# One load cut in two, and two early products put behind the head matmuls, in a one-token attention block

## The chip, the core and the metric

The kernel runs on one NeuronCore of a Trainium2 chip. The core has five engines that run side by side and meet at semaphores: TensorE (PE) for matmuls, VectorE (DVE), ScalarE (ACT), GpSimd (POOL) and SyncE (SP), which here only issues transfers. Sixteen DMA engines carry data between the chip's main memory and the on-chip tile memory of 128 partitions. The metric is the device time of one execution in microseconds (us). The times of before are 1310.05 us as the median of three runs (1310.01 to 1310.16).

## The reference

One token of each of two sequences is decoded. The input is layer-normed. One branch is attention of 32 query heads over 8 cached key/value heads, each with 32,768 positions of 128 numbers; the other is a small gated feed-forward. Their product is added to the input.

```python
xn = layernorm(x)                                   # x: 2 x 1 x 512
q = (xn @ wq).reshape(B, 1, 32, 128)                # wq: 512 x 4096
k, v = repeat(k_cache, 4), repeat(v_cache, 4)       # caches: 2 x 8 x 32768 x 128, float32
p = softmax(einsum("bhqd,bhkd->bhqk", q, k) * 128 ** -0.5)
s = einsum("bhqk,bhkd->bhqd", p, v).reshape(B, 1, 4096) @ wo      # wo: 4096 x 512
gate = xn @ W_gate                                  # 512 x 1792
h = gate * (gate > 0) * (xn @ W_up)
out = x + s * silu(h @ W_down)                      # W_down: 1792 x 512
```

Everything is float32. The caches are two times 268 MB, and each number of them is used once.

## The kernel before

The caches are read in loads of 8 MB: a load is one row of 16,384 numbers (64 KB) for each of the 128 partitions. The two sequences and eight key/value heads make 16 groups; a group is four tiles of 8,192 positions, and a load brings two tiles. So there are 32 loads of keys (tiles `k0` and `k1` by turns) and 32 of values (tile `w`, which the code calls `wide`; the last but one goes into `k0`).

The step `j` of the main loop (L882) works on one pair of tiles. DVE turns the keys in 32 by 32 blocks (L660), PE multiplies them by the query (`s<-k,qcur`), DVE takes the scores (L678), ACT exponentiates a whole group (L722), PE and DVE bring the weights into the layout that the values need (`pt`, `wt`), and PE sums the values (`o<-w,wt` or `o<-k,wt`) two steps later. At the end of a group, DVE adds the four parts of the sum into `ob` (L771, L777), four head matmuls (`m_ps<-ob,heads`) spread it by heads, DVE turns that (L803), and POOL stores it in `ots` (L812), where the heads of all groups stand until the projection by `wo`.

Nothing sets the order at run time. The `Program` class records each operation with the tiles that it reads and writes (by key), and works out from these which semaphore each operation waits for; within an engine the order is that of the recording. All large loads stand on SP's queue. `load` (L239) records a transfer with a semaphore of its own name, and a load into a tile waits until the last readers of its key are through.

The beginning. The first operation of all (L261) is the load of the query weights `wq`, 8 MB, into `w`; the second is the first load of keys. ACT's queue loads `x` twice, 4 KB each (L289, L290). DVE and POOL prepare constants, DVE makes the layer norm (L364 to L380), PE turns it (L391), DVE copies it to `wt0` (L401), and `project_q` (L456) multiplies it by the query weights; it waits for `wt0` and `w`. After that `w` is free for the weights of the feed-forward.

The end. In the last but one step the last values are loaded, and then `load_wo` (L439) brings the output weights into `k1` in six pieces: the first half of `wo` in one piece of 4 MB, the second in pieces of 2 MB, 1 MB, 512 KB, 256 KB and 256 KB, each with its own semaphore. `project_near` (L826) takes the output projection in products of four matmuls, each of the four on its own 32 columns of PE: product `n` needs rows of `ots` and one piece of `wo`. Seven products add up in one bank, `s0`. Products 0 to 3 need the first half of `wo` and heads that were done long before; products 4 to 6 need the heads of the last group too. DVE copies the bank (L846), and `project_far` (L848) adds the remaining pieces of `wo` and the folded copy in a second bank. DVE multiplies by the gate (L870) and adds the input (L872), and SP writes the result.

In the last step the order is this (L911 to L919): `sums`, `take_o` (which makes `ob`), products 0 to 3, `finish_group` (the head matmuls, L803 and L812), and, behind the loop, products 4 to 6 (L936).

## Time and profile before

| what | value |
|---|---|
| median of three runs | 1310.05 us (1310.01 to 1310.16) |
| the profiled execution | 1309.84 us |
| its span, first to last instruction | 1308.2 us |
| mean granted clock of TensorE | 0.836 |
| read from main memory | 564.67 MB, 432 GB/s over the span |
| busy: PE, DVE, ACT, POOL | 65%, 55%, 4%, 1% |
| DMA packets | 10692 |

Times in the profile count from the start of the span. An engine's busy time says how long its instructions took, not that the kernel waited for them: the chain that ended last shows that. A row of a group gives the line, engine, operation, the tile written and those read, the count, the busy time, and what ended the idle time before it. Buffer numbers are left out, so `k` is `k0` or `k1` and `s` one of the two banks of scores, which the end of the kernel uses for the output projection.

### The profile page before, as it was taken

The page shows a single profiled execution, that of the slowest core. Times are in us where ns is not written, and L with a number is a line of the kernel's source. Part 1 is how long each engine was busy: PE and PEld are TensorE (multiplying, and loading weights), DVE is VectorE, ACT ScalarE, POOL GpSimd, SP SyncE. Part 2 cuts the span into 40 slices and gives each one's busy share as a digit, 9 for nine tenths or more (in the row PEclk, how much of TensorE's full clock was granted, in tenths as well). Part 3 has the DMA queues.
Part 4 walks back from the last instruction along what each step waited for, and adds up shares of the span by engine and source line. Part 5 has one row for each costly group of instructions (what it writes and reads, how often), then busy time and mean ns, then how long its engine had stood idle before and what let it go on. Part 6 is the DMA issues. An engine that isn't in the chain of part 4 may idle for free.

```text
span 1308.2 us, 11146 instructions
## 1 busy us (share of the span) xinstructions
PE 850.1 (65%) x4720; PEld 211.5 (16%) x4720; DVE 718.0 (55%) x690; ACT 51.4 (4%) x133; POOL 10.5 (1%) x38
## 2 busy tenths in 40 slices
PE   3566565766666586566667656676665657666676
PEld 0211111111111121111211111121111112111122
DVE  2666654565655456664546666455665545656521
ACT  0001000000000000000000000000000000000000
POOL 0000000000000000000000000000000000000000
PEclk9777888897788888777887878788878888977888
DMA  9999999999999999999999999999999999999998
GB/s 417 419 438 441 439 427 439 429 439 427 439 427 441 427 439 441 429 441 429 435 431 437 429 439 429 437 439 429 443 431 435 431 437 429 439 427 439 435 433 361
DMA packets 10692, 564.79 MB, mean 432 GB/s; under 512 B 1194, under 2 KB 1210, under 8 KB 1596
## 3 DMA queue, kind: packets, MB, share of 16 engines
q1 hardware_dynamic: 10668, 564.67, 99.7%
q8 instruction: 6, 0.10, 0.0%
q14 instruction: 2, 0.02, 0.0%
q10 hardware_dynamic: 16, 0.01, 0.0%
HBM read 564.67 MB, written 0.00 MB: 432 GB/s over the span
## 4 chain that ended last, share of the span: by engine, by line
DMA 63%; DVE 18%; PE 15%; issue 4%; SPq 0%; POOL 0%
DMA k<-in_A_k_cache_dram 58%; DVE k L660 18%; PE o L243 8%; PE s L243 6%; DMA k<-in_A_wo_dram 3%; DMA w<-in_A_wq_dram 2%; PE m_ps L243 1%; PE m_ps L693 0%; SPq L240 0%; DVE os L803 0%; DVE os L846 0%; DVE gy L870 0%; DVE gy L872 0%; POOL ots L812 0%
## 5 line engine op out<-in xcount | busy, mean ns | idle before, releaser
L243 PE MATMUL s<-k,qcur 128*32 128x512 f32 x2048 | 491.5, 687 | 377.0 <-DVE k L660 376.9
L660 DVE STREAM_TRANSPOSE k<-k 128x2048 f32<-128x2048 f32 x256 | 565.2, 2275 | 148.4 <-DMA k<-in_A_k_cache_dram 148.4
L243 PE MATMUL o<-w,wt 128*16 128x512 f32 x1984 | 244.8, 595 | 7.9 <-DMA w<-in_A_v_cache_dram 7.9
L243 PEld LDWEIGHTS s<-k,qcur 128*32 128x32 f32 x2048 | 87.7, 120 | 782.2 <-DVE k L660 645.2
L737 DVE STREAM_TRANSPOSE wt<-pt 128x512 f32<-128x512 f32 x64 | 45.9, 717 | 145.0 <-PE pt L243 140.7
L678 DVE TENSOR_SCALAR_CACHE_REDUCE st<-s 128x512 f32<-128x512 f32 x64 | 43.0, 672 | 113.4 <-PE s L243 113.4
L243 PEld LDWEIGHTS o<-w,wt 128*16 128x16 f32 x1984 | 62.7, 97 | 165.5 <-issue 165.5
L722 ACT ACTIVATE st<-st,nb 128x512 f32<-128x512 f32 x64 | 45.4, 710 | 1109.1 <-DVE nb L719 1109.1
L243 PE MATMUL pt<-st,perm 128*128 128x512 f32 x128 | 75.4, 720 | 1.5 <-ACT st L722 1.5
L763 DVE RECIPROCAL rl<-m_ps 128x1 f32<-128x1 f32 x16 | 2.7, 168 | 109.3 <-PE m_ps L243 109.3
L243 PE MATMUL m_ps<-ob,heads 128*128 128x128 f32 x128 | 21.7, 320 | 29.0 <-DVE ob L777 29.0
L243 PEld LDWEIGHTS pt<-st,perm 128*128 128x128 f32 x128 | 26.0, 225 | 35.0 <-issue 30.7
L803 DVE STREAM_TRANSPOSE os<-m_ps 128x512 f32<-128x512 f32 x16 | 11.5, 717 | 25.6 <-PE m_ps L243 25.6
L243 PEld LDWEIGHTS m_ps<-ob,heads 128*128 128x128 f32 x128 | 18.0, 217 | 31.1 <-DVE ob L777 30.3
L243 PE MATMUL m_ps<-w,wt 128*32 128x512 f32 (+1 forms) x128 | 17.0, 666 | 8.3 <-DMA w<-in_A_wq_dram 8.3
L777 DVE SCALAR_TENSOR_TENSOR ob<-o,share,ob 128x128 f32<-128x128 f32 x48 | 16.9, 351 | 1.7
L530 POOL TENSOR_TENSOR qcur<-qall,block_of 128x128 f32<-128x128 f32 x16 | 6.5, 406 | 1008.4 <-PE s L243 972.6
L243 PE MATMUL o<-k,wt 128*16 128x512 f32 x64 | 9.5, 757 | 4.5 <-DMA k<-in_A_v_cache_dram 4.5
L243 PE MATMUL m_ps<-negone,mrow 1*128 1x1 f32 x32 | 6.0, 256 | 9.3 <-DVE mrow L708 9.3
L722 ACT ACTIVATION_READ_ACCUMULATOR st<-st,nb 128x1 f32 x64 | 12.0, 187 | 0.0
L481 DVE COPY os<-m_ps 128x512 f32<-128x512 f32 x2 | 1.4, 691 | 17.3 <-PE m_ps L243 17.3
L391 PE MATMUL m_ps<-ident,st 32*128 32x32 f32 x4 | 0.7, 308 | 14.0 <-DVE st L380 14.0
(80 smaller groups left out, 103.1 us busy)
## 6 DMA issues: line engine op xcount, KB each, us to landing
k<-in_A_wo_dram SPq DMA_DIRECT2D x1, 4096.0 KB, 39.1
w<-in_B_W_gate_dram SPq DMA_DIRECT2D x1, 3584.0 KB, 18.5
w<-in_B_W_up_dram SPq DMA_DIRECT2D x1, 3584.0 KB, 26.6
w<-in_B_W_down_dram SPq DMA_DIRECT2D x1, 3584.0 KB, 17.3
k<-in_A_wo_dram SPq DMA_DIRECT2D x1, 2048.0 KB, 43.4
k<-in_A_wo_dram SPq DMA_DIRECT2D x1, 1024.0 KB, 45.4
k<-in_A_k_cache_dram SPq DMA_DIRECT2D x32, 48.6
k<-in_A_wo_dram SPq DMA_DIRECT2D x1, 512.0 KB, 46.2
```

The lines of the kernel that those rows point to most:

```text
L243: return lambda e: e.matmul(out_, lhs, rhs, start=start, stop=stop, skip_group_check=True)
L391: lambda e, k=k: e.transpose(px[:, k * 32 : (k + 1) * 32], xquad[:, k, :], ident[:32, :32])
L481: dve(lambda e, q=qs, h=half: e.tensor_copy(q, pq[h]), [f"m{half}"], [f"os{half}"])
L530: lambda e: e.tensor_tensor(qcur.rearrange("p e (k h) -> p e k h", h=REP), qall[:, b, hk].unsqueeze(2).to_broadcast([P, 4, Q // REP, REP]) ...
L660: dve(lambda e: e.transpose(at_, at_), [f"k{t // 2 % 2}"], [key])
L678: lambda e: e.tensor_scalar(st[u], ps_s[t % 2], SCALE, None, op0=ALU.mult, op1=ALU.max, accum_out=mx[:, u : u + 1],),
L722: lambda e, u=u: e.activation(st[u], st[u], AF.Exp, bias=nb, scale=1.0, accum_out=ls[:, u : u + 1]),
L737: dve(lambda e: e.transpose(wt[t % 2], ps_p[t % 2]), [f"pt{t % 2}"], [f"wt{t % 2}"])
L763: dve(lambda e: e.reciprocal(rl, ps_m[1][:, :1]), ["m1"], ["rl"])
L777: lambda e, part=part, c=c: e.scalar_tensor_tensor(ob, part, share[:, c : c + 1], ob, op0=ALU.mult, op1=ALU.add),
L803: lambda e: e.transpose(ot, ps_m[1].rearrange("p (h q j) -> p j h q", h=REP, j=ROWS)),
```

## The change

The load of the query weights becomes two: partitions 0 to 15 with a semaphore `wq0`, and partitions 16 to 127 with the semaphore `wq`. The second writes a key of its own, `wide_rest`, so that it does not wait for the first; `project_q` reads both keys. And in the last step two of the early products, not four, stand ahead of `finish_group`; products 2 and 3 come behind it, with 4 to 6.

```diff
+FIRST = 16
...
-    load(wide, wq.rearrange("(p k) n -> p (k n)", k=NKC), "wq", w=["wide"])
+    wq_rows = wq.rearrange("(p k) n -> p (k n)", k=NKC)
+    load(wide[:FIRST], wq_rows[:FIRST], "wq0", w=["wide"])
+    load(wide[FIRST:], wq_rows[FIRST:], "wq", w=["wide_rest"])
...
-                ["wt0", "wide"],
+                ["wt0", "wide", "wide_rest"],
                 [f"m{half}"],
...
                 take_o()
                 if not live:
-                    project_near(range(4))
+                    project_near(range(2))
                 finish_group(j // 2 - 1)
...
-    project_near(range(4, NEAR))
+    project_near(range(2, NEAR))
     project_far()
```

SP's queue at the start of the program, before (each row is a transfer: tile, source, partitions x numbers):

```order
L240 DMA w<-in_A_wq_dram 128x16384
L240 DMA k<-in_A_k_cache_dram 128x16384
L240 DMA w<-in_B_W_gate_dram 128x7168 [waits sem_PE]
L240 DMA w<-in_B_W_up_dram 128x7168
L240 DMA k<-in_A_k_cache_dram 128x16384
```

The same place after the change, where all lines have moved down by one:

```order
L241 DMA w<-in_A_wq_dram 16x16384
L241 DMA w<-in_A_wq_dram 112x16384
L241 DMA k<-in_A_k_cache_dram 128x16384
L241 DMA w<-in_B_W_gate_dram 128x7168 [waits sem_PE]
L241 DMA w<-in_B_W_up_dram 128x7168
L241 DMA k<-in_A_k_cache_dram 128x16384
```

One row became two, neither of which waits; everything behind stands one place later.

PE at the end of the program, from the sums of the last group on, before (`s<-k,ots` are the products by the output weights, four rows each; `m_ps<-ob,heads` are the head matmuls):

```order
L243 MATMUL m_ps<-lcol,same 128x1 [waits sem_DVE]
L243 MATMUL s<-k,ots 32x512 [waits sem_wo0_0]
L243 MATMUL s<-k,ots 32x512 x15
L243 MATMUL m_ps<-ob,heads 128x128 [waits sem_DVE]
L243 MATMUL m_ps<-ob,heads 128x128 x3
L243 MATMUL s<-k,ots 32x512 [waits sem_wo1_0,sem_POOL]
L243 MATMUL s<-k,ots 32x512 x7
L243 MATMUL s<-k,ots 32x512 [waits sem_wo1_8]
L243 MATMUL s<-k,ots 32x512 x3
```

The same place after the change:

```order
L244 MATMUL m_ps<-lcol,same 128x1 [waits sem_DVE]
L244 MATMUL s<-k,ots 32x512 [waits sem_wo0_0]
L244 MATMUL s<-k,ots 32x512 x7
L244 MATMUL m_ps<-ob,heads 128x128 [waits sem_DVE]
L244 MATMUL m_ps<-ob,heads 128x128 x3
L244 MATMUL s<-k,ots 32x512 x8
L244 MATMUL s<-k,ots 32x512 [waits sem_wo1_0,sem_POOL]
L244 MATMUL s<-k,ots 32x512 x7
L244 MATMUL s<-k,ots 32x512 [waits sem_wo1_8]
L244 MATMUL s<-k,ots 32x512 x3
```

Eight matmuls, which wait for nothing new, went from ahead of the head matmuls to behind them; the products that wait for POOL and the later pieces of `wo` kept their order.

## The prediction

> **What bounds the kernel now.** I read the page first: the share of each engine, the DMA line of the forty slices, and the chain of work that ended last.

> ```profile
> PE 850.1 (65%) x4720; PEld 211.5 (16%) x4720; DVE 718.0 (55%) x690; ACT 51.4 (4%) x133; POOL 10.5 (1%) x38
> DMA  9999999999999999999999999999999999999998
> GB/s 417 419 438 441 439 427 439 429 439 427 439 427 441 427 439 441 429 441 429 435 431 437 429 439 429 437 439 429 443 431 435 431 437 429 439 427 439 435 433 361
> DMA 63%; DVE 18%; PE 15%; issue 4%; SPq 0%; POOL 0%
> ```

> No compute engine is above 65%, while the sixteen DMA engines are at 90% or more in every slice but the last. The DMA share by stage (the last two numbers of each row are that share and the GB/s) makes this sharper:

> ```profile
> 43.00:83.00 40.00, 21.27 (x130) 5.92 (x130) 25.79 (x19) 0.00 (x0) 0.00 (x0) 0.80 1.01 435
> 83.00:640.00 557.00, 372.88 (x2033) 88.24 (x2032) 322.11 (x293) 22.90 (x61) 4.46 (x14) 0.83 1.00 435
> 640.00:1250.00 610.00, 403.44 (x2165) 98.72 (x2169) 349.54 (x314) 22.69 (x63) 4.48 (x15) 0.83 1.00 434
> ```

> From 43 to 1250 us the transfer engines have no hole to give back. 435 GB/s over 16 engines is 27.2 GB/s each. A row of one partition (16384 floats, 65,536 bytes, one packet) so takes 65,536 / 27.2 GB/s = 2.41 us, and a load of 128 rows, eight packets per engine, 19.3 us. Next, how far ahead of need the transfers are issued:

> ```profile
> k<-in_A_k_cache_dram SPq DMA_DIRECT2D x32, 48.6
> w<-in_A_v_cache_dram SPq DMA_DIRECT2D x31, 29.7
> w<-in_A_wq_dram SPq DMA_DIRECT2D x1, 22.1
> ```

> A load of 19.3 us that lands 48.6 or 29.7 us after its issue has stood in the queue behind another for at least 10 us. So time lost by the DMA engines is not made up anywhere: whatever the slowest of them loses at the start comes out at the end, one for one, and so does whatever it gains. I therefore price the first edit in DMA engine time and the second by what waits in the last 13 us.

> **The first load: what it removes.** The packets are counted where they begin; these are the first slices with any (again share and GB/s last):

> ```profile
> 1.50:2.00 0.50, 0.00 (x0) 0.00 (x0) 0.42 (x8) 0.00 (x0) 0.00 (x0) 1.00 3.58 1180
> 2.00:2.50 0.50, 0.00 (x0) 0.00 (x0) 0.20 (x4) 0.00 (x0) 0.00 (x0) 1.00 1.82 655
> 2.50:3.00 0.50, 0.00 (x0) 0.00 (x0) 0.45 (x1) 0.00 (x0) 0.00 (x0) 1.00 0.30 131
> 3.00:3.50 0.50, 0.00 (x0) 0.00 (x0) 0.39 (x2) 0.23 (x1) 0.00 (x0) 1.00 0.33 131
> ```

> 1180 GB/s for 0.5 us is 590 KB, nine packets; then 5, 1 and 1 (131 GB/s is one). So sixteen engines begin one after another, the last some 1.0 to 1.5 us after the first. A first transfer with one packet per engine can let all begin together. Gain: at least 0, at most 1.3 us (the spread). I take 0.3, because fourteen of the sixteen begin within the first us, and the engine that begins last is the last at the end only if no other is held up later.

> **What it adds.** One more DMA on SP's queue, ahead of the first key load:

> ```profile
> 0.74 0.39 SPq L240 DMA_DIRECT2D w<-in_A_wq_dram  x1
> 1.19 0.41 SPq L240 DMA_DIRECT2D k<-in_A_k_cache_dram  x1
> 0.74 22.13 DMA w<-in_A_wq_dram
> 23.01 10.05 PE m_ps L243 x64
> ```

> The key load is issued about 0.45 us later, at 1.64, and its first packet is not due before the query weights are through at about 22.5: 20 us of cover, cost 0. Only with that cover gone would it cost the 0.45. PE waits for one semaphore more ahead of the query projection, which starts when the last part lands; nothing else is queued there that could run. The two small loads of x on ACT's queue share the DMA engines with these packets:

> ```profile
> 10.19 0.67 DVE L364 TENSOR_REDUCE stat<-st 32x1 f32<-32x512 f32 x1 [2.98 <-DMA st<-in_A_x_dram]
> 14.77 0.29 DVE L401 COPY wt<-m_ps 128x128 f32<-128x128 f32 x1 [0.78 <-PE m_ps L391]
> 23.01 10.00 PE L243 MATMUL m_ps<-w,wt 128*32 128x512 f32 x64 [8.28 <-DMA w<-in_A_wq_dram]
> ```

> x arrives by 10.19 and the normalised activations are ready at 15.06, 8 us before the weights. If first packets become longer, x comes later by about as much as the weights, so this stays covered.

> **What it moves: where the sixteen engines write.** This is the term that decides. In every large load of the trace sixteen engines write all 128 partitions at once. In the new first transfer they all write partitions 0 to 15. No row shows such a transfer, so I bound it. From below: each engine is bound by itself, the packet stays at 2.41 us, cost 0. From above: if the tile's way in is shared out by partitions, eight neighbours to a way (the 128 partitions over sixteen engines' worth of rate), sixteen partitions have two ways, eight engines share each, and the first packets take 8 x 2.41 = 19.3 us: 16.9 us lost. Between these, with neighbours in fours the sixteen engines have four ways and lose 3 x 2.41 = 7.2 us; in twos they lose 2.4. No row is near either end; I take 7.2, the rung nearest the middle (8.4) of 0 and 16.9.

> [...]

> The second transfer has 112 rows, seven per engine. From below: as in the whole loads, nobody meets, 0. From above: sixteen neighbours in each of seven steps, 7 x 7.2 = 50.7 us. Between: each engine takes seven rows that lie together, so at any moment the engines stand seven rows apart, in sixteen different fours of the 32. Two fours share a way; the partner of a four is then in use with chance 15/31 = 0.48, and a packet that meets another takes up to 2.41 us more: 7 x 2.41 x 0.48 = 8.2 us. I take 5, nearer to this than to the whole loads' 0, because engines that met fall out of step and meet for part of a packet only. What remains is kept for the range.

> **The two products moved at the end.** These are the rows of the last 13 us, and the landing times of the output weights:

> ```profile
> 1256.35 2.81 SPq L240 DMA_DIRECT2D k<-in_A_wo_dram  x6
> 1295.38 1.12 DVE L777 SCALAR_TENSOR_TENSOR ob<-o,share,ob 128x128 f32<-128x128 f32 x3
> 1295.45 3.64 PE L243 MATMUL s<-k,ots 128*32 128x512 f32 x32 [0.96 <-DMA k<-in_A_wo_dram]
> 1299.02 1.16 PE L243 MATMUL m_ps<-ob,heads 128*128 128x128 f32 x8
> 1300.21 0.72 DVE L803 STREAM_TRANSPOSE os<-m_ps 128x512 f32<-128x512 f32 x1 [3.71 <-PE m_ps L243]
> 1300.99 0.21 POOL L812 COPY ots<-os 32x16 f32<-32x16 f32 x1 [39.64 <-DVE os L803]
> 1301.26 1.50 PE L243 MATMUL s<-k,ots 128*32 128x512 f32 x12 [1.08 <-POOL ots L812]
> 1302.76 0.37 PEld L243 LDWEIGHTS s<-k,ots 128*32 128x32 f32 x8 [0.48 <-DMA k<-in_A_wo_dram]
> 1304.11 0.69 DVE L846 COPY os<-s 128x512 f32<-128x512 f32 x1 [3.18 <-PE s L243]
> 1305.79 0.29 DVE L870 TENSOR_TENSOR gy<-s,gy 128x128 f32<-128x128 f32 x1 [0.99 <-PE s L243]
> k<-in_A_wo_dram SPq DMA_DIRECT2D x1, 2048.0 KB, 43.4
> k<-in_A_wo_dram SPq DMA_DIRECT2D x1, 1024.0 KB, 45.4
> k<-in_A_wo_dram SPq DMA_DIRECT2D x2, 256.0 KB, 46.4
> ```

> ob is done at 1296.50, but the head matmuls wait behind four products and start at 1299.02. A product costs (1299.02 - 1295.45)/4 = 0.89 us. With two ahead the heads start at 1297.24, 1.78 earlier, and POOL has written ots by 1299.42 instead of 1301.20. The two moved products then run from 1298.4 to 1300.2, in PE's old idle time (1.08 us before 1301.26). What is late next is the data. The six issues take 2.81 us, one each 0.476: the 2048 KB piece is issued at 1256.83 and lands at 1300.2, the 1024 KB piece at 1257.30 and lands at 1302.7, the last at 1258.73 and lands near 1305.1. So products five and six run from 1300.2 to 1302.0, and the seventh starts at 1302.76, with its data. Now PE works without a break from 1301.26 to 1304.09, and the seventh starts after two products, at about 1303.0. The copy thus moves from 1304.11 to about 1303.87: 0.24 us at most, and at least 0, if the last pieces bind. I take 0.2.

> **Sum.** +7.2 +5.0 -0.3 -0.2 = +11.7 us on the profiled execution's own 1309.84 (span 1308.2 and 1.6 around it): 1321.5. The median of the runs is 0.2 above that execution, so 1321.7.

> **Rivals.** First, no meeting: the engine alone limits a packet. For it: packets keep their rate in all stages, 434 to 435 GB/s, and nothing in this trace shows a shared way; against it: no row has sixteen engines on few partitions. Then -0.3 -0.2 = -0.5, 1309.5; with the whole start-up spread gone 1308.5; with nothing gained 1310.0. It decides as soon as the 16-row transfer lands within 5 us of its issue. Not slower; chance 0.31, nearly all within 0.2%. It includes the case that the edit does not do what it says, because another engine is last at the end.

> Second, neighbours in twos: +2.4 and little in the second transfer, about 1312.5 (1311.5 to 1316): 0.05.

> Third, the 112 rows are dealt out in turn, so that every step is like the first: +7.2 x 8 = 57.9, 1367.5. For it: nothing; against it: the whole loads are dealt so that nobody meets. 0.06.

> Fourth, faster by over 0.2% (2.6 us): start-up spread and tail together give at most 1.3 + 0.24 = 1.5, so something unseen must help: 0.02.

> **Numbers.** 0.2%, 2.6 us, is about what a measurement of this kernel can tell from no change. The forecast (a loss of 6 to 18 us) has 0.56, and its own range is 1316 to 1328: the first packets alone from below; from above 7.2 + 8.2 and some engine held up besides, or the full 16.9. The whole range runs down to the first rival, 1309.0 to 1328.0, and leaves out about 0.1. Slower: 0.56 + 0.06 + 0.04 of the twos = 0.66; same: 0.30 + 0.02 = 0.32; faster 0.02.

> **What would show it.** In the DMA issues the 1 MB transfer should take about 10 to 12 us to land, not 4 to 5, and the rest of the query weights should land near 34, not 22.9. The first of the forty slices should show about 300 GB/s or less instead of 417, the middle ones 435 as now, and the chain should end with the same pieces later by the same amount. The seventh product should start with its DMA, and the head matmuls right behind the second. A 1 MB transfer that lands in under 5 us makes the forecast wrong; so does a landing of the query weights before 25 us, or a second transfer that takes several times its 17 us.

## The result, and the profile after

The change makes the kernel slower: 1330.88 us (median of five runs, 1330.51 to 1331.85) against 1310.05, a ratio of 1.016 with a 95% interval of 1.0148 to 1.0171. That is 20.8 us more; 11.7 had been forecast, and the range ended at 1328.0.

The page of the changed kernel, as for before: shares of the engines, the DMA line and the rate in forty slices, the chain.

```profile
PE 855.0 (64%) x4720; PEld 211.1 (16%) x4720; DVE 718.2 (54%) x690; ACT 51.4 (4%) x133; POOL 10.5 (1%) x38
DMA  9999999999999999999999999999999999999998
GB/s 217 364 433 445 434 426 436 440 432 428 438 436 436 426 438 436 436 430 436 434 440 432 432 434 438 436 428 436 438 434 428 438 436 436 428 438 434 436 430 346
DMA 64%; DVE 18%; PE 14%; issue 4%; SPq 0%
```

The DMA engines are as busy as before in every slice, yet in the first (33 us long) they move 217 GB/s instead of 417: busy, but at half speed. From the third slice to the last but one the rates lie where they lay (426 to 445 GB/s, against 427 to 443 before), and the stage from 83 to 640 us has its share of 1.00 and 434 GB/s, against 435:

```profile
83.00:640.00 557.00, 371.29 (x1993) 89.45 (x1989) 318.61 (x285) 22.15 (x58) 4.08 (x13) 0.82 1.00 434
```

So the loss lies at the start, and what is lost there is carried to the end. The chain over the first 80 us, then the row for the landing times of the loads into `w` that were issued up to 60 us (the shortest and the longest are the two transfers of the query weights):

```profile
1.21 42.77 DMA w<-in_A_wq_dram
44.11 8.44 PE m_ps L244 x64
DMA to landing us min/median/max: 12.0/23.2/42.8
```

The 1 MB transfer lands 12.0 us after its issue, and all the weights at 1.21 + 42.77 = 43.98, where they landed at 0.74 + 22.13 = 22.87 before. These 21.1 us are the 21.2 by which the span grew (1329.4 against 1308.2).

The single packets can be read too. A packet is counted in the stretch in which it begins, and in this load the engines begin their packets nearly together. In a stretch that holds just sixteen packets (350 GB/s for 3 us is 1.05 MB, sixteen times 65,536 bytes) the DMA share, the number before the last, times the length of the stretch is the mean time of a packet. First the kernel before, its first three packets:

```profile
1.00:4.00 3.00, 0.00 (x0) 0.00 (x0) 2.27 (x15) 0.73 (x1) 0.29 (x1) 1.00 1.01 350
4.00:6.00 2.00, 0.00 (x0) 0.00 (x0) 1.83 (x9) 0.56 (x1) 0.00 (x0) 1.00 1.21 524
7.00:9.00 2.00, 0.00 (x0) 0.00 (x0) 0.21 (x1) 0.00 (x0) 0.00 (x0) 1.00 1.22 527
```

That is 3.0 us for the first (start-up included) and 2.4 for the others. The changed kernel, all eight packets and the first of the key load behind them:

```profile
1.00:3.00 2.00, 0.00 (x0) 0.00 (x0) 1.57 (x13) 0.00 (x0) 0.29 (x1) 1.00 4.27 524
9.00:12.00 3.00, 0.00 (x0) 0.00 (x0) 0.00 (x0) 0.00 (x0) 0.00 (x0) 1.00 1.82 350
15.00:17.00 2.00, 0.00 (x0) 0.00 (x0) 0.00 (x0) 0.00 (x0) 0.00 (x0) 1.00 2.34 527
19.00:21.00 2.00, 0.00 (x0) 0.00 (x0) 0.00 (x0) 0.00 (x0) 0.00 (x0) 1.00 1.61 525
23.00:26.00 3.00, 0.47 (x4) 0.47 (x4) 2.01 (x5) 1.49 (x2) 0.00 (x0) 1.00 1.27 350
27.00:30.00 3.00, 0.00 (x0) 0.00 (x0) 0.00 (x0) 0.00 (x0) 0.00 (x0) 1.00 1.50 350
31.00:34.00 3.00, 0.00 (x0) 0.00 (x0) 0.00 (x0) 0.00 (x0) 0.00 (x0) 1.00 1.55 350
35.00:39.00 4.00, 0.00 (x0) 0.00 (x0) 0.00 (x0) 0.00 (x0) 0.00 (x0) 1.00 1.12 262
40.00:43.50 3.50, 0.00 (x0) 0.00 (x0) 0.00 (x0) 0.00 (x0) 0.00 (x0) 1.00 0.85 300
```

The packets take 8.5, then 5.5, 4.7, 3.2, 3.8, 4.5, 4.7 and 4.5 us, and the first of the keys 3.0. By these means the first transfer costs 8.5 - 3.0 = 5.5 us, the seven packets of the second 30.8 - 16.9 = 13.9, and the keys behind them 0.6: 20.0 in all. The weights land with the slowest engine, 21.1 us later than before.

### The profile page after: what moved, and what is told of

It reads as the page before. It is cut to its first block, busy times and chain, and to the rows that moved or that the text cites. A ratio compares the mean times of both kernels' runs of the same rounds, so it can differ in the third digit from the quotient of the medians.

```text
span 1329.4 us, 11147 instructions
## 1 busy us (share of the span) xinstructions
PE 855.0 (64%) x4720; PEld 211.1 (16%) x4720; DVE 718.2 (54%) x690; ACT 51.4 (4%) x133; POOL 10.5 (1%) x38
## 2 busy tenths in 40 slices
DMA  9999999999999999999999999999999999999998
## 4 chain that ended last, share of the span: by engine, by line
DMA 64%; DVE 18%; PE 14%; issue 4%; SPq 0%
DMA k<-in_A_k_cache_dram 58%; DVE k L663 18%; PE o L244 8%; PE s L244 5%; DMA k<-in_A_wo_dram 3%; DMA w<-in_A_wq_dram 3%; PE m_ps L244 1%; PE m_ps L696 0%; SPq L241 0%; DVE gy L873 0%; DVE gy L875 0%
## 5 line engine op out<-in xcount | busy, mean ns | idle before, releaser
L244 PE MATMUL s<-k,qcur 128*32 128x512 f32 x2048 | 497.1, 696 | 372.9 <-DVE k L663 372.8
L725 ACT ACTIVATE st<-st,nb 128x512 f32<-128x512 f32 x64 | 45.4, 710 | 1110.2 <-DVE nb L722 1110.2
L806 DVE STREAM_TRANSPOSE os<-m_ps 128x512 f32<-128x512 f32 x16 | 11.5, 718 | 23.6 <-PE m_ps L244 23.6
L244 PEld LDWEIGHTS m_ps<-ob,heads 128*128 128x128 f32 x128 | 18.0, 217 | 31.1 <-DVE ob L780 31.1
L780 DVE SCALAR_TENSOR_TENSOR ob<-o,share,ob 128x128 f32<-128x128 f32 x48 | 16.9, 351 | 1.7
## 6 DMA issues: line engine op xcount, KB each, us to landing
w<-in_B_W_up_dram SPq DMA_DIRECT2D x1, 3584.0 KB, 27.2
k<-in_A_wo_dram SPq DMA_DIRECT2D x1, 2048.0 KB, 43.4
k<-in_A_wo_dram SPq DMA_DIRECT2D x1, 1024.0 KB, 45.4
k<-in_A_k_cache_dram SPq DMA_DIRECT2D x32, 48.6
```

The lines of the kernel that those rows point to most:

```text
L244: return lambda e: e.matmul(out_, lhs, rhs, start=start, stop=stop, skip_group_check=True)
L725: lambda e, u=u: e.activation(st[u], st[u], AF.Exp, bias=nb, scale=1.0, accum_out=ls[:, u : u + 1]),
L780: lambda e, part=part, c=c: e.scalar_tensor_tensor(ob, part, share[:, c : c + 1], ob, op0=ALU.mult, op1=ALU.add),
L806: lambda e: e.transpose(ot, ps_m[1].rearrange("p (h q j) -> p j h q", h=REP, j=ROWS)),
```

## The experiments

### The two parts apart

The tail alone (the first load in one piece):

```diff
-                    project_near(range(4))
+                    project_near(range(2))
...
-    project_near(range(4, NEAR))
+    project_near(range(2, NEAR))
```

> The kernel before with the two products moved behind the head matmuls, and the query weights in one load. If the last pieces of the output weights bind the end, as the trace of the changed kernel suggests (the last of its products waits for DMA, and from the landing of the first piece to the end of the last addition it takes 10.95 us as before): no change, within 0.1 us of 1310.0. If PE's order bound the end, as the prediction had it: 0.2 us faster.

Measured: 1309.9 against 1310.1, ratio 0.9998 (0.9989 to 1.0007): no change that can be told. The end of its trace:

```profile
1296.93 1.12 DVE L777 SCALAR_TENSOR_TENSOR ob<-o,share,ob 128x128 f32<-128x128 f32 x3
1298.10 0.97 PEld L243 LDWEIGHTS m_ps<-ob,heads 128*128 128x128 f32 x8 [1.12 <-DVE ob L777]
1302.93 0.16 PEld L243 LDWEIGHTS s<-k,ots 128*32 128x32 f32 x8 [1.01 <-DMA k<-in_A_wo_dram]
1304.07 0.69 DVE L846 COPY os<-s 128x512 f32<-128x512 f32 x1 [4.05 <-PE s L243]
1305.41 0.16 PEld L243 LDWEIGHTS s<-k,ots 128*32 128x32 f32 x8 [0.22 <-DMA k<-in_A_wo_dram]
1305.91 0.29 DVE L870 TENSOR_TENSOR gy<-s,gy 128x128 f32<-128x128 f32 x1 [1.15 <-PE s L243]
```

The reordering works: the head matmuls start right behind `ob` (1298.05), where they stood 2.5 us behind it before. (In this execution `ob` itself came 1.55 us later than in the one profiled before, so the price of the step is read from the ratio and not from these rows.) But the seventh product then waits for its piece of `wo`, and the last matmuls wait for the last piece. The time moved from PE's order into waits for data.

The first load alone:

```diff
+FIRST = 16
...
-    load(wide, wq.rearrange("(p k) n -> p (k n)", k=NKC), "wq", w=["wide"])
+    wq_rows = wq.rearrange("(p k) n -> p (k n)", k=NKC)
+    load(wide[:FIRST], wq_rows[:FIRST], "wq0", w=["wide"])
+    load(wide[FIRST:], wq_rows[FIRST:], "wq", w=["wide_rest"])
...
-                ["wt0", "wide"],
+                ["wt0", "wide", "wide_rest"],
```

> The query weights in two loads, 16 partitions and 112, and the end as before. All theories that put the loss into the first load: +20.8 us, 1330.9, as the whole change. If the moved products lost something too, less than that.

Measured: 1331.42, ratio 1.0159 (1.0144 to 1.0175). The whole loss is here.

### Other cuts

The same 1 MB first, but cut by columns, so that both transfers reach all 128 partitions:

```diff
+FIRST = 2048
...
-    load(wide, wq.rearrange("(p k) n -> p (k n)", k=NKC), "wq", w=["wide"])
+    wq_rows = wq.rearrange("(p k) n -> p (k n)", k=NKC)
+    load(wide[:, :FIRST], wq_rows[:, :FIRST], "wq0", w=["wide"])
+    load(wide[:, FIRST:], wq_rows[:, FIRST:], "wq", w=["wide_rest"])
...
```

> The first load cut by columns: the same 1 MB first, but as the first 2,048 numbers of all 128 partitions, then the rest of all of them. Shared ways into the tile (partitions in fours share a way, and two transfers of all partitions meet nowhere): within 0.5 us of 1310.0. If it is the cut itself that costs, one transfer more with its own landing: near the +20.8 us of the change, or at least several us.

Measured: 1310.4, ratio 1.0 (0.9991 to 1.001). The landings, in us from issue:

```profile
w<-in_A_wq_dram SPq DMA_DIRECT2D x1, 7168.0 KB, 21.3
w<-in_A_wq_dram SPq DMA_DIRECT2D x1, 1024.0 KB, 4.9
```

The same bytes in the same two sizes land in 4.9 us instead of 12.0. This cut costs nothing that can be measured, and a first transfer that lands early brings nothing either.

Two halves, 64 partitions each (the edit is to the run with the first load alone):

```diff
-FIRST = 16
+FIRST = 64
```

> The first load cut into partitions 0 to 63 and 64 to 127, four rows for each engine twice, both powers of two. Shared ways: rows four apart by engine, so the engines e and e+8 stand 32 partitions apart in all eight steps; if the partner of a four stands 32 partitions from it, every packet takes twice 2.41 us, 8 x 2.41 = 19.3 us lost, 1329.3. If each partition has a way of its own and the odd numbers 16 and 112 are to blame: within 1 us of 1310.0.

Measured: 1331.59, ratio 1.0162 (1.0146 to 1.0177), 21.5 us lost where 19.3 had been expected. Four of its eight packets:

```profile
1.00:4.00 3.00, 0.00 (x0) 0.00 (x0) 2.27 (x15) 0.60 (x1) 0.29 (x1) 1.00 1.58 350
6.00:8.00 2.00, 0.00 (x0) 0.00 (x0) 1.18 (x7) 0.00 (x0) 0.00 (x0) 1.00 2.57 524
11.00:13.00 2.00, 0.00 (x0) 0.00 (x0) 0.00 (x0) 0.00 (x0) 0.00 (x0) 1.00 2.58 527
16.00:18.00 2.00, 0.00 (x0) 0.00 (x0) 0.00 (x0) 0.00 (x0) 0.00 (x0) 1.00 2.57 525
```

The first takes 4.7 us, the other three 5.1 us each, twice 2.4 and a little more. The numbers 16 and 112 are not to blame: two even halves lose as much (21.5 us against the 21.3 of the cut into 16 and 112), as they would if each half reached half of the ways. In rate, 16 x 65,536 bytes in 5.14 us are 204 GB/s, where the loads of all partitions run at 435.

### An extra transfer of 1 MB, put in four places

These are the kernel before with one transfer ahead of the query weights, into a key tile that is free then and overwritten by its own load later. The first is the control, with all partitions; in the others only the line of the probe differs:

```diff
-    load(wide, wq.rearrange("(p k) n -> p (k n)", k=NKC), "wq", w=["wide"])
+    wq_rows = wq.rearrange("(p k) n -> p (k n)", k=NKC)
+    load(kbuf[1][:, :2048], wq_rows[:, :2048], "probe", w=["k1"])
+    load(wide, wq_rows, "wq", w=["wide"])
```

> The kernel before with an extra transfer of 1 MB ahead of the query weights, into a tile that is free then and overwritten later: 2,048 numbers of all 128 partitions. This prices the bytes alone: 1 MB at 435 GB/s is 2.4 us, so +2.4 us, 1312.5, by all theories.

Measured: 1312.8, ratio 1.0019 (1.0009 to 1.0028), 2.6 us for the bytes. Then neighbours, partitions 0 to 15:

```diff
+    load(kbuf[1][:16], wq_rows[:16], "probe", w=["k1"])
```

> The same extra 1 MB, but as rows of 64 KB into partitions 0 to 15. Shared ways: the packets take about 8.9 us as the first ones of the changed kernel, so 2.4 + 6.0 = 8.4 us, 1318.5; the rest of the weights in one load costs nothing. If the loss of the change came from the 112 rows alone: +2.4, 1312.5.

Measured: 1319.87, ratio 1.0072 (1.0054 to 1.009), 9.7 us, where 8.4 had been expected. Then every fourth partition from 32 on, with the same source:

```diff
+    load(kbuf[1][32:96:4], wq_rows[:16], "probe", w=["k1"])
```

> The same 16 rows of 64 KB from the same place in memory into partitions 32, 36, ... 92, four apart. Shared ways, with fours 32 apart as partners: sixteen different ways, nobody meets, +2.4 us, 1312.5. If sixteen rows of adjacent memory read at once are slow, or a transfer of sixteen packets as such: +8.4 us, 1318.5, as into neighbouring partitions.

Measured: 1313.33, ratio 1.0025 (1.0015 to 1.0035), 3.1 us. And neighbours again, from every eighth row of the source:

```diff
+    load(kbuf[1][:16], wq_rows[::8], "probe", w=["k1"])
```

> Sixteen rows into partitions 0 to 15 again, but read from every eighth row of the weights, spread over 8 MB of memory. Shared ways into the tile: as with adjacent rows, +8.4 us, 1318.5. If adjacent memory is the cause: +2.4 us, 1312.5.

Measured: 1319.47, ratio 1.007 (1.0052 to 1.0088), 9.3 us. The first packets with neighbours, and then with partitions four apart:

```profile
1.00:4.00 3.00, 0.00 (x0) 0.00 (x0) 2.26 (x15) 0.72 (x1) 0.29 (x1) 1.00 2.83 350
```

```profile
1.00:4.00 3.00, 0.00 (x0) 0.00 (x0) 2.26 (x15) 0.72 (x1) 0.29 (x1) 1.00 0.94 350
```

The mean is 8.5 us against 2.8 for the same packets. Where they come from changes little (9.3 against 9.7 us in all); where they go decides. The source and the small transfer as such are out.

### Who pays when two engines meet

Two engines meet, in the words of the theory, when they write at the same time through one way. No row shows a way. That it serves two fours, groups of four neighbouring partitions each, is the author's assumption; the halves agree with it, sixteen fours at 204 GB/s where all 32 run at 435. Two rows 32 partitions apart do not always slow each other. In the run with partitions four apart eight pairs stood so (32 and 64, 36 and 68, up to 60 and 92), each with one row below partition 64 and one from 64 on, and the sixteen packets took 2.8 us on the mean. None of its pairs lay 32 apart within one half of the 128 partitions, so that is the distance tried next. Shifted by two partitions, one pair of rows falls so (30 and 62); shifted by eight, two pairs do (24 and 56, 28 and 60):

```diff
+    load(kbuf[1][30:94:4], wq_rows[:16], "probe", w=["k1"])
```

> Sixteen rows of 64 KB ahead of the query weights again, into partitions 30, 34, ... 90. With fours 32 apart as partners, one pair of engines meets (partitions 30 and 62) and fourteen engines have ways of their own. Ways shared by those alone who meet: two engines take about 4.8 us for the first packet and fourteen 2.4 to 3.1 as into 32, 36, ... 92, so about fourteen second packets begin by 5.5 us; the end waits for the slow pair, +2.4 us against that run, 1315.7. A meeting that holds up all engines: hardly a second packet before 6 us. No such partners: 1313.3 as that run.

```diff
+    load(kbuf[1][24:88:4], wq_rows[:16], "probe", w=["k1"])
```

> The same into partitions 24, 28, ... 84: two pairs meet (24 and 56, 28 and 60) and twelve engines have ways of their own. Shared by those alone who meet: four engines slow, about twelve second packets begin by 5.5 us; end +2.4 us against the run without a meeting, 1315.7. A meeting holds up all, as the 4.7 us of all sixteen packets in most steps of the changed kernel suggests: hardly a second packet before 6 us, with the same end.

Measured: 1314.81 with one pair (1.0035, 1.0021 to 1.005) and 1315.51 with two (1.0043, 1.0026 to 1.0059), 4.7 and 5.4 us over the kernel before, so 1.6 and 2.3 more than the 3.1 without such a pair, where 2.4 had been expected. The first sixteen packets and the stretch in which the second begin, with one pair and then with two:

```profile
1.00:4.00 3.00, 0.00 (x0) 0.00 (x0) 2.26 (x15) 0.73 (x1) 0.29 (x1) 1.00 1.05 350
5.00:6.00 1.00, 0.00 (x0) 0.00 (x0) 0.86 (x7) 0.00 (x0) 0.00 (x0) 1.00 2.30 852
```

```profile
1.00:4.00 3.00, 0.00 (x0) 0.00 (x0) 2.27 (x15) 0.73 (x1) 0.29 (x1) 1.00 1.51 350
5.00:6.00 1.00, 0.00 (x0) 0.00 (x0) 0.86 (x7) 0.00 (x0) 0.00 (x0) 1.00 0.00 0
```

With one pair the mean is 3.15 us, little over the 2.8 without such a pair, and 852 GB/s for 1 us, thirteen packets, begin between 5 and 6 us: the others are hardly held up. With two pairs the mean is 4.5 us and not one packet begins between 5 and 6. Four engines that took 4.8 us and twelve that took 2.8 would give 3.3; if the four took 4.8, the other twelve took 4.4 on the mean. So, if the pairs are counted rightly, two meetings at once hold up engines that meet nobody. Each theory was right for one of the two runs.

The second transfer alone, as the last test:

```diff
+    load(kbuf[1][16:], wq_rows[16:], "probe", w=["k1"])
```

> The second transfer of the change alone: 112 rows into partitions 16 to 127 of the free tile, ahead of the query weights in one load. Its bytes alone take 16.9 us (7 packets of 2.41 per engine). By the changed kernel's trace, where they took about 33: +33 us, 1343. If the 112 rows were only slow because the 16 before them had put the engines out of order: +17 to +20, 1327 to 1330. Chance meetings as in the prediction: +22 to +25, 1332 to 1335.

Measured: 1341.14, ratio 1.0237 (1.022 to 1.0254), 31.1 us for bytes that take 16.9 at 2.41 us a packet. The loss of about 14 belongs to the 112 rows themselves, whatever stood before them. The first four steps of sixteen packets:

```profile
1.00:3.00 2.00, 0.00 (x0) 0.00 (x0) 1.57 (x13) 0.00 (x0) 0.29 (x1) 1.00 2.20 524
5.00:8.00 3.00, 0.00 (x0) 0.00 (x0) 2.03 (x13) 0.00 (x0) 0.00 (x0) 1.00 1.59 350
10.00:13.00 3.00, 0.00 (x0) 0.00 (x0) 0.00 (x0) 0.00 (x0) 0.00 (x0) 1.00 1.21 351
14.00:16.20 2.20, 0.00 (x0) 0.00 (x0) 0.87 (x3) 0.00 (x0) 0.00 (x0) 1.00 1.42 477
```

They take 4.4, 4.8, 3.6 and 3.1 us: the third and fourth are short here too, as in the changed kernel.

## Why the prediction was right and wrong

**Right: the place, the sign, and the one-for-one carrying.** The loss was put into the ways by which neighbouring partitions are reached, and the runs agree: neighbours 8.5 us from adjacent rows of the source and 8.6 from every eighth, partitions four apart from 32 on 2.8. Time lost in the first load came out at the end, 21.1 of 21.2 us. The forecast's sign for the first packets was read where it was said to show: 12.0 us to land, and the first slice at half the rate.

**The first packets: right in kind and near in size.** Of 0, 2.4, 7.2 and 16.9 the rung for neighbours in fours was taken. By the traces that was luck: it was taken because it lay nearest the middle, and no row of before spoke for it. The mean packet lost 5.5 us against the first packet of before. At the end, where the slowest engine counts, the 1 MB transfer to neighbours cost 6.5 us more than the one to partitions four apart (1319.87 against 1313.33) and 7.1 more than the one to all partitions (1312.8). In the changed kernel the transfer's packets begin between 1 and 3 us and are over between 9 and 12, where the next ones begin; sixteen packets of 8.5 us are 123 GB/s, where the loads of all partitions run at 435.

**Wrong: the seven packets of the second transfer, the +5.** This term is the step that failed: the weights landed at 44 us and not near 34. It multiplied 2.41 us by the chance that an engine meets another, 0.48, got 8.2, and then took 5 "because engines that met fall out of step and meet for part of a packet only". No run shows that: in the changed kernel the sixteen packets of each of the eight steps begin within a stretch of 2 to 4 us that holds no other. That two fours share a way was assumed in it and stood in no row of before; of the runs, the halves at 204 GB/s agree with it. The term measured 13.9 by the packets' mean, and 31.1 - 16.9 = 14.2 with the 112 rows alone; with the 7.1 of the first packets that is 21.3, the whole of the loss. Two things were wrong in it. Meetings were taken as chance, though by the theory they can be counted: with seven consecutive rows per engine, and fours 32 partitions apart within one half as partners, the seven packets have 2, 2, 1, 1, 2, 2 and 2 pairs that meet (16 with 51 and 72 with 107 in the first, and so on). That is only 24 of 112 packets, 0.21 and not 0.48. And only those who meet were charged, though with two pairs the others pay too (4.5 us on the mean of all sixteen). Measured against the count, the two packets with one pair take 3.2 and 3.8 us, and the five with two pairs 4.5 to 5.5; with the 112 rows alone, the first four take 4.4, 4.8, 3.6 and 3.1 for 2, 2, 1 and 1 pairs. That engines take consecutive rows, and which fours are partners, is inferred from this agreement and from the two runs with pairs, not seen in a row.

**Wrong: the upper bound.** 7.2 + 8.2 and some engine held up besides, or 16.9 for the first transfer alone, was taken as the most in the range. But 8.2 was an average over engines, and the load lands with its slowest engine (21.1 us later, 20.0 by the mean packets). If every step lasts as long as its worst pair, the bound is seven packets at twice the time, 16.9 more, and with 7.2 that is 24.1: the range would have reached 1334 and held 1330.9.

**The start-up term, +0.3 gained: not seen.** With all first packets slow there was nothing to read it from, and the cut by columns, which reaches all partitions, is not faster than before (1310.4 against 1310.1). The nearest run is the 1 MB transfer to partitions four apart, sixteen packets of 2.8 us on the mean: all second packets then begin within one us (5 to 6), but it cost 3.1 us where its bytes take 2.4, so no gain shows there either.

**The tail, 0.2 gained: its lower bound, 0, came true.** The working had named the case "if the last pieces bind", and they do (0.9998 with the tail alone, the last matmuls behind the landing of the last piece).

**The rivals.** No meeting (0.31) falls with the run of neighbours against four apart (8.5 us against 2.8); twos fall with the 8.5 us; rows dealt in turn (0.06) falls too, since 8.5 us in each of seven steps would be 59.5, and the second transfer alone took 31.1. The covers held: `x` came at 21.68, 11.5 us later, and its chain ended 17 us before the weights landed.

```profile
21.68 0.67 DVE L367 TENSOR_REDUCE stat<-st 32x1 f32<-32x512 f32 x1 [14.45 <-DMA st<-in_A_x_dram]
26.26 0.29 DVE L404 COPY wt<-m_ps 128x128 f32<-128x128 f32 x1 [0.78 <-PE m_ps L394]
44.11 8.40 PE L244 MATMUL m_ps<-w,wt 128*32 128x512 f32 x64 [17.89 <-DMA w<-in_A_wq_dram]
```

## What to carry to other kernels

Where the DMA engines are the bound, as here, cut a load by columns and not into blocks of neighbouring partitions: the same 1 MB landed in 4.9 us over all partitions and in 12.0 over sixteen neighbours, and even two halves of 64 partitions ran at half the rate (204 GB/s against 435). It is the neighbours that cost and not the number of partitions: sixteen of them four apart cost 3.1 us from partition 32 on, near the 2.6 of all 128, and 4.7 and 5.4 from 30 and from 24 on, against 9.7 for sixteen neighbours. A DMA share of 1.00 does not say that the engines move what they can (1.00 at 217 GB/s while the two halves come in, 1.00 at 435 from 83 to 640 us before): read it together with the GB/s. And where a step lasts as long as its worst member, its bound is the worst case, not a mean over chances.

## What the runs showed of the hardware that had not been expected

One pair of rows 32 apart within one half (partitions 30 and 62) cost the other fourteen next to nothing (3.15 us per packet on average against 2.8), but with two pairs at once (24 and 56, 28 and 60) the mean of all sixteen was 4.5 us. The two runs differ also in where the rows lie within their fours; the steps of the 112 rows, where that changes from step to step, show the same order (3.1 to 3.8 us with one pair, 4.4 to 5.5 with two). Why the second pair would hold up engines that are in no pair is not settled: the profile has no row for what an engine waits on inside a packet. Two halves of 64 partitions took 5.1 us per packet behind the first, a little over twice the 2.4 of a load that reaches all partitions: 5.14 against 2 x 2.41 = 4.82, some 6% more; the first packet, 4.7 us, does not show it.
